# A planned RWKV + MLP kernel: new planner constants, a charge for changing the kind of matmul, and the diagonal terms of four units on GpSimd

## The chip, the cores and the metric

The kernel runs on one core of one Trainium2 chip. The metric is the device time of one execution in microseconds, smaller is better; the median of three runs of the kernel before is 541.37 us (541.27 to 541.45).

## The reference

An RWKV recurrence over 768 tokens (batch 4, 8 heads, head size 48), and behind it an MLP with an ELU in the middle (384 to 2048 to 384) on the 3072 tokens that come out.

```python
for t in range(S):
    cur = np.einsum('bhd,bhe->bhde', u[None] * kt, vt)
    y[:, :, t] = np.einsum('bhd,bhde->bhe', rt, state + cur)
    state = wt[:, :, :, None] * state + np.einsum('bhd,bhe->bhde', kt, vt)
...
h = x @ w_in
g = np.where(h > 0.0, h, alpha * (np.exp(np.minimum(h, 0.0)) - 1.0))
return g @ w_out
```

## The kernel before, in words

The sequence is cut into 6 chunks of 128 tokens; a chunk and a batch make a unit, so there are 24 units, 0 to 23, four to a chunk (units 0 to 3 are chunk 0, units 4 to 7 chunk 1, and so on). The units of chunks 2, 3 and 4 work in two halves of 64 tokens (HALVES).

A unit's attention is a chain of steps over all engines. VectorE makes two running products of the decays (`es`, `gs`: L377, L387) and scales r and k with them (`rh`, `kh`: L392, L396). The diagonal term, the sum of r times k times u for each head and token, becomes the small tile `md`. It is made in one of two ways. With DIAG "PE", VectorE multiplies r by k (`rkc`, L416), TensorE sums with u by small matmuls (`pd`, L421), ScalarE copies the sum out (`md`, L425). With DIAG "POOL", another copy of r and k by token (`rk`, 384 KB a unit) is loaded, GpSimd multiplies r by k and by u (L404, L407), and VectorE sums for each head (`md`, L411). Then `md` is spread on a diagonal (`sp`): on ScalarE for units 0 to 7 (L432), on GpSimd for the others (L442). TensorE makes the scores (`s`, L456), VectorE lays them over the diagonal (`mk`, L460), TensorE transposes k (`t`, L465; ScalarE copies it out, `kt`, L469), makes the outputs (`v`, L493 to L506; `ya` is the part of it that takes the state) and the state's update (`u`, L532), VectorE brings the state up to date (`sc`, `up`: L472, L540, L542), and the output is split in a high and a low part for fp32r matmuls (`xh`, `xl`: L513, L519).

The MLP goes by chunk and by f, the 16 blocks of 128 hidden units: `g1` (9 matmuls of 512 columns, L238), ReLU and exponential on ScalarE (L243, L246), ELU on VectorE (`stt`, L249), the split (`gh` L253 on ScalarE, `gl` L257 on VectorE), and `g2` (9 matmuls, L268). In chunks 0 and 1 the first six f are done in two halves of 256 columns. Each f needs its weights once, in a high and a low part: they are loaded in chunk 0 and worked up by ScalarE and VectorE (`a`, `cand`, `cb`, `cc`, `wh`, `wl`: L559 to L577).

The order on every engine's queue is written down at build time by `Plan.order()`, a list scheduler. Each step has an assumed duration (COST), and a latest time `late`, which runs backwards from due times: `g1` and `g2` of chunk c are due along the line from BEGINS[c] to BEGINS[c+1], and `v` of a unit at BEGINS[c] less STAG (half units) or STAG_C (others, chunks 2 and up) for each unit of its chunk that follows. At each moment every engine takes, of the steps that are ready and whose buffers are free, the one with the smallest `late` (L143). STAY is added to a step of TensorE if it would change between attention and MLP, SWITCH to the time that TensorE is taken when the kind of step changes (L168), and HALF is a time up to which TensorE is assumed at half speed (L166). `lock` says that VectorE and GpSimd are assumed not to run such steps at once. Only the order goes into the kernel; on the chip each queue waits by semaphores. Scores take two of three PSUM tiles "pa" until `mk`, `u` of a half unit two of them until `up2` and `xl` (L707, L713); the loads of a chunk's units may start LEAD before BEGINS (L599).

Of the kernel before, what the change touches and what calls it, by code (L numbers as in the profile page):

```python
# [8 lines left out]
F32 = mybir.dt.float32  # L9
# [4 lines left out]
AF = mybir.ActivationFunctionType  # L14
ALU = mybir.AluOpType
# [35 lines left out]
PIECES = _pieces()  # L51


COST = dict(es=1.5, gs=1.4, pc=0.2, pd=0.6, md=0.22, spa=2.4, rh=0.62, kh=0.62, rk=0.48, rku=0.48, prk=1.1, prku=1.1, dg=0.5, mk=0.7, up=0.7, sc=0.5, xl=0.48,
            cand=0.5, cv=0.9, wl=0.9, stt=0.6, gl=0.64, fl=1.4, kt=0.5, xh=0.46, a=0.87, wh=0.8, r1=0.58, r2=0.6, gh=0.6,
            sp=1.7, s=1.15, t=0.5, v=1.75, v0=1.1, u=0.5, g=2.06, out=0.6, sh=0.6, ya=0.4, vh=1.0)
LAT = 0.06
DMA_FIRST, DMA_ISSUE, DMA_LAT, DMA_RATE = 1.0, 0.45, 1.9, 215.0
BEGINS = (20.9, 120.4, 207.5, 284.8, 361.5, 453.5, 461.1)
SOON = 0.0  # L60
HALF = 0.0
STAY = 0.0
SWITCH = 0.0
MODES = dict(s=1, v=2, u=3, pd=4)
STAG = 10.9
STAG_C = 0.0
HALVES = (2, 3, 4)
FIRST = "DVE"
FILL = {}
COLS = 128  # L70
PAD = 96
LEAD = 69.5
DIAG = ["PE"] * 8 + ["POOL"] * 16
SPREAD = ["ACT"] * 8 + ["POOL"] * 16
SLOTS = dict(w=2, k=3, r=3, rk=2, v=4, eg=2, md=2, am=2, kt=1, pa=3, wg=2, ph=2, m=2, gh=2, gl=2, x=2, acc=1, raw0=1, x0=1, x1=1, x1a=1, x1b=1)

# [1 line left out]
class Plan:  # L78
# [5 lines left out]
    def add(self, key, eng, dur, fn, after=(), due=None, start=0.0, lock=False, size=0):  # L84
        self.tasks[key] = dict(key=key, eng=eng, dur=dur, fn=fn, after=list(after), due=due, start=start, lock=lock, size=size)
# [8 lines left out]
    def order(self):  # L94
# [14 lines left out]
        for k in reversed(topo):  # L109
            t = ts[k]  # L110
# [4 lines left out]
        users = {}  # L115
        ring = {p: [0, [False] * n] for p, n in SLOTS.items()}
        free = lambda p, n: not any(ring[p][1][(ring[p][0] + x) % len(ring[p][1])] for x in range(n))
        ready = {e: [] for e in ("PE", "DVE", "ACT", "POOL", "SP")}
        count = {k: len(t["after"]) for k, t in ts.items()}
        at = {k: t["start"] for k, t in ts.items()}  # L120
        rank = {k: n for n, k in enumerate(ts)}
# [2 lines left out]
        server, mode = DMA_FIRST, None  # L124
# [5 lines left out]
        while len(order) < len(ts):  # L130
            moved = False
            for e in ready:
                if busy[e] > now + 1e-9:
                    continue
                best = None
                for k in ready[e]:
                    t = ts[k]
                    if at[k] > now + 1e-9 or any(
                            not free(p, n) or (p in turn and turn[p][0] != k) for p, n, _ in self.holds.get(k, ())):
                        continue  # L140
                    if t["lock"] and max(v for x, v in locked.items() if x != e) > now + 1e-9:
                        continue
                    u = (t["late"] + (STAY if e == "PE" and (k[0] in MODES) != (mode in MODES) else 0.0), rank[k])  # L143
                    if best is None or u < best[0]:
                        best = u, k
                if best is None:
                    continue
                k = best[1]
                t = ts[k]
                ready[e].remove(k)  # L150
                for p, n, us in self.holds.get(k, ()):
                    at_, n_ = ring[p][0], len(ring[p][1])
                    ring[p][0] = (at_ + n) % n_
# [12 lines left out]
                end = now + t["dur"] * (2.0 if e == "PE" and now < HALF else 1.0)  # L166
                if e == "PE":
                    end += SWITCH * (MODES.get(mode, 0) != MODES.get(k[0], 0))  # L168
                    mode = k[0]
                busy[e] = end  # L170
                if t["lock"]:
                    locked[e] = end
                if e == "SP":
                    server = max(server, end) + t["size"] / DMA_RATE / 1e3
                    end = server + DMA_LAT
                t["began"], t["ended"] = now, end
                events.append((end, k))
                order.append(k)
                moved = True
# [112 lines left out]
def rwkv_elu_kernel(ctx, tc, wkr, rk, vp, u, uz, gkrw, gv, gu, w_in, w_out, out):  # L292
    nc = tc.nc
# [16 lines left out]
    tt, stt, act = nc.vector.tensor_tensor, nc.vector.scalar_tensor_tensor, nc.scalar.activation  # L310
# [4 lines left out]
    w_h = big.tile([P, NF, 2, NK, P], F32R, name="w_h")  # L315
    w_l = big.tile([P, NF, 2, NK, P], F32R, name="w_l")
# [16 lines left out]
    raws, xts = {}, {}  # L333
# [253 lines left out]
    add, hold, K = plan.add, plan.hold, COST  # L587
# [9 lines left out]
    for u_ in units:  # L597
# [44 lines left out]
            after.append(("v", i - 1))  # L642
        more = 0.15 * u_["half"]
        if u_["half"]:
            add(("u", i), "PE", K["u"], lambda u_=u_: outer(u_), [("kt", i)] + after[:3])
            add(("ya", i), "PE", K["ya"], lambda u_=u_: state_part(u_, 0), [("u", i), ("sc", i)])
            add(("up", i), "DVE", K["up"], lambda u_=u_: update(u_), [("ya", i)])
            add(("sc2", i), "DVE", K["sc"], lambda u_=u_: scale_state(u_, 1), [("up", i)], lock=True)
            add(("v", i), "PE", K["vh"], lambda u_=u_: value(u_), after + [("sc2", i)], due=BEGINS[c] - (B - 1 - b) * STAG - 2.0)
            add(("up2", i), "DVE", K["up"], lambda u_=u_: update(u_, 1), [("xl", i)])  # L650
        else:
            add(("v", i), "PE", K["v" if c else "v0"], lambda u_=u_: value(u_), after, due=BEGINS[c] - (B - 1 - b) * STAG_C - 1.0 if c > 1 else None)
# [5 lines left out]
    for f in range(NF):  # L658
        for z in range(2):
            add(("raw", f, z), "SP", DMA_ISSUE, lambda f=f, z=z: load_w(f, z), [("raw", f, 0)] if z else [("raw", f - 1, 1)], size=393)  # L660
        add(("a", f), "ACT", K["a"], lambda f=f: conv_a(f), [("raw", f, 0), ("raw", f, 1)])
        add(("cand", f), "DVE", K["cand"], lambda f=f: conv_and(f), [("a", f)], lock=True)
        add(("cb", f), "DVE", K["cv"], lambda f=f: conv_b(f), [("cand", f)], lock=True)
        add(("cc", f), "DVE", K["cv"], lambda f=f: conv_c(f), [("cb", f)], lock=True)
        add(("wh", f), "ACT", K["wh"], lambda f=f: conv_h(f), [("cc", f)])
        add(("wl", f), "DVE", K["wl"], lambda f=f: conv_l(f), [("wh", f)], lock=True)
    n0, prev = 0, None
    seq = []
    for c in range(NC):
# [186 lines left out]
```

## Time and profile before

| | |
|---|---|
| median of 3 runs | 541.37 us |
| the profiled execution: its time, its span | 543.14 us, 540.9 us |
| mean granted clock of TensorE | 0.974 |
| busy: TensorE matmuls, weight loads | 515.5 us (95%), 427.7 us (79%) |
| busy: VectorE, ScalarE, GpSimd | 371.1 us (69%), 285.8 us (53%), 74.7 us (14%) |
| chain that ended last, by engine | TensorE 80%, VectorE 9%, DMA 6%, ScalarE 2% |

The execution's own time is 2.24 us over its span. The busy time of TensorE is modelled from the starts of matmuls, so slow or spread-out matmuls count as busy too; how long a group of nine takes from its start to the next start says more. The table is a mean over stages; the rows below show the stages.

### The profile page before, as it was taken

Reading aid. Unit: us, or ns where it says so; the run is one execution under the profiler, and the core shown is the slowest. Engines: PE = TensorE matmul, PEld = TensorE weight load, DVE = VectorE, ACT = ScalarE, POOL = GpSimd, SP = SyncE. Lnnn points to the kernel's source line nnn. Section 1 sums busy time; section 2 is a strip of 40 time slices with the busy share of each in tenths; the row PEclk is TensorE's granted clock in tenths of the full one; section 3 lists DMA queues with packets and bytes.
Section 4 is the critical chain, followed back from the end, with each engine's and each line's share of the span. In section 5 each row is a group of like instructions: output and inputs, shape, how many; then the busy total and the mean of one; then the engine's idle time right before and its main releaser. Section 6 shows DMA issues by size and latency. Waiting matters only on the chain.

```text
span 540.9 us, 12202 instructions
## 1 busy us (share of the span) xinstructions
PE 515.5 (95%) x5121; PEld 427.7 (79%) x5121; DVE 371.1 (69%) x614; ACT 285.8 (53%) x570; POOL 74.7 (14%) x102
## 2 busy tenths in 40 slices
PE   6876999989999999999999999999999999999994
PEld 5666998878999777787777788777788887888883
DVE  5899899988778875469964478964436995333331
ACT  3768588675855453455453365543355543454441
POOL 2000000000243120028120035120031400000000
PEclk9977899979999999999999999999999999999998
DMA  8954754021562200094310083100084110010001
GB/s 243 287 176 141 226 175 164 19 56 35 175 178 76 65 2 2 2 263 133 85 33 2 3 241 103 35 2 3 1 254 124 48 35 2 0 60 0 1 0 63
DMA packets 26749, 47.54 MB, mean 88 GB/s; under 512 B 2753, under 2 KB 9281, under 8 KB 26689
## 3 DMA queue, kind: packets, MB, share of 16 engines
q1 hardware_dynamic: 26544, 46.58, 28.7%
q8 instruction: 42, 0.69, 0.5%
q14 instruction: 19, 0.15, 0.1%
q10 hardware_dynamic: 144, 0.13, 0.1%
HBM read 41.98 MB, written 4.72 MB: 86 GB/s over the span
## 4 chain that ended last, share of the span: by engine, by line
PE 80%; DVE 9%; DMA 6%; ACT 2%; issue 1%; SPq 0%; DVEq 0%; ACTq 0%
PE ph L238 34%; PE acc L268 33%; PE pa_s L456 3%; PE pa_y L501 3%; DMA v<-in_vp_dram 3%; PE pa_u L506 2%; PE pa_u L493 2%; PE pa_u L532 1%; DMA wrawx<-in_w_out_dram 1%; DMA rk<-in_rk_dram 1%; PE pa_t L465 1%; DVE eg L387 1%; DVE gl L257 1%; DMA k<-in_wkr_dram 1%; DVE r L392 1%
## 5 line engine op out<-in xcount | busy, mean ns | idle before, releaser
L243 ACT ACTIVATE m<-ph 128x512 f32<-128x512 f32 (+1 forms) x108 | 59.2, 549 | 132.8 <-PE ph L238 131.5
L249 DVE SCALAR_TENSOR_TENSOR m<-m,ph 128x512 f32<-128x512 f32 (+1 forms) x108 | 67.4, 624 | 84.7 <-ACT m L246 84.2
L238 PE MATMUL ph<-xh,w_h 128*128 128x512 f32 (+1 forms) x324 | 123.2, 380 | 2.0 <-ACT w_h L574 1.6
L238 PE MATMUL ph<-xh,w_l 128*128 128x512 f32 (+1 forms) x324 | 120.7, 372 | 3.7 <-DVE w_l L577 3.7
L268 PE MATMUL acc<-gh,w_h 128*128 128x512 f32 (+1 forms) x325 | 123.6, 380 | 0.0
L268 PE MATMUL acc<-gl,w_h 128*128 128x512 f32 (+1 forms) x325 | 120.2, 370 | 0.1
L238 PE MATMUL ph<-xl,w_h 128*128 128x512 f32 (+1 forms) x324 | 120.1, 371 | 0.0
L268 PE MATMUL acc<-gh,w_l 128*128 128x512 f32 (+1 forms) x325 | 119.9, 369 | 0.0
L257 DVE TENSOR_TENSOR gl<-m,gh 128x512 fp32r<-128x512 f32 (+1 forms) x108 | 73.2, 681 | 36.4 <-ACT gh L253 35.9
L253 ACT CAST gh<-m 128x512 fp32r<-128x512 f32 (+1 forms) x108 | 61.5, 571 | 55.9 <-DVE m L249 33.2
L238 PEld LDWEIGHTS ph<-xh,w_l 128*128 128x128 f32 x324 | 62.3, 192 | 15.0 <-DVE w_l L577 4.6
L238 PEld LDWEIGHTS ph<-xh,w_h 128*128 128x128 f32 x324 | 62.2, 192 | 14.3 <-ACT w_h L574 2.4
L268 PEld LDWEIGHTS acc<-gh,w_h 128*128 128x128 f32 x325 | 62.4, 192 | 12.8 <-issue 1.0
L268 PEld LDWEIGHTS acc<-gh,w_l 128*128 128x128 f32 x325 | 62.4, 192 | 10.2
L268 PEld LDWEIGHTS acc<-gl,w_h 128*128 128x128 f32 x325 | 62.5, 192 | 9.7 <-DVE gl L257 0.5
L238 PEld LDWEIGHTS ph<-xl,w_h 128*128 128x128 f32 x324 | 62.5, 193 | 9.4
L246 ACT ACTIVATE m<-m 128x512 f32<-128x512 f32 (+1 forms) x108 | 63.3, 586 | 2.9
L442 POOL TENSOR_SCALAR_AFFINE_SELECT am<-md 64x256 f32<-64x256 f32 (+1 forms) x56 | 30.5, 548 | 96.9 <-PE pa_u L493 61.9
L404 POOL TENSOR_TENSOR rk<-rk 128x384 f32<-128x384 f32 x16 | 19.1, 1192 | 134.1 <-DMA rk<-in_rk_dram 132.2
L377 DVE TENSOR_TENSOR_SCAN eg<-w,reset 112x516 f32<-112x516 f32 (+1 forms) x24 | 31.0, 1292 | 2.6 <-DMA w<-in_wkr_dram 2.6
L456 PE MATMUL pa_s<-r,k 48*64 48x64 f32 (+1 forms) x576 | 27.3, 262 | 5.5 <-ACT md L425 2.2
L401 ACT ACTIVATE junk<-eg,lim 112x1032 bf16<-112x1032 f32 (+1 forms) x24 | 27.7, 1153 | 8.2 <-DVE eg L387 8.2
(72 smaller groups left out, 513.4 us busy)
## 6 DMA issues: line engine op xcount, KB each, us to landing
v<-in_vp_dram SPq DMA_DIRECT2D x24, 256.0 KB, 6.5
rk<-in_rk_dram SPq DMA_DIRECT2D x16, 384.0 KB, 4.1
w<-in_wkr_dram SPq DMA_DIRECT2D x24, 227.9 KB, 3.9
k<-in_wkr_dram SPq DMA_DIRECT2D x24, 224.0 KB, 4.9
r<-in_wkr_dram SPq DMA_DIRECT2D x24, 224.0 KB, 5.3
out_dram<-o SPq DMA_DIRECT2D x17, 256.0 KB, 2.5
wrawx<-in_w_in_dram SPq DMA_DIRECT2D x10, 384.0 KB, 3.5
wrawx<-in_w_out_dram SPq DMA_DIRECT2D x10, 384.0 KB, 4.1
```

Source lines behind the costliest of these rows:

```text
L238: nc.tensor.matmul(ph[z:z + COLS], w[:, f, 0, k, z:z + COLS], x_[:, k, :], start=(k == n == 0), stop=(k == NK - 1 and n == 2))
L243: act(s["m"], s["ph"], AF.Relu, scale=-1.0)
L246: act(s["m"], s["m"], AF.Exp, scale=-1.0)
L249: stt_(s["m"], s["m"], -1.0, s["ph"], ALU.add, ALU.max)
L253: nc.scalar.copy(s["gh"], s["m"])
L257: nc.vector.tensor_tensor(s["gl"], s["m"], s["gh"].bitcast(F32), ALU.subtract)
L268: nc.tensor.matmul(a_[z:z + COLS], w[:, f, 1, m, z:z + COLS], g[:, s_], start=(f == n == 0 and lo == 0), stop=(f == NF - 1 and q == parts ...
L377: nc.vector.tensor_tensor_scan(out=eg[:, 0, 0:n][:, ::-1], data0=u_["w"][:, 1:n + 1][:, ::-1], data1=reset[:, 0, 0:n][:, ::-1], initial=0. ...
L401: act(junk[:, :, 0:n], u_["eg"][:, :, 0:n], AF.Relu, bias=lim, accum_out=flags[:, u_["i"]:u_["i"] + 1])
L404: eng.tensor_tensor(u_["rk"][:, 0], u_["rk"][:, 0], u_["rk"][:, 1], ALU.mult)
L442: nc.gpsimd.affine_select(out=am[rs, :, 0:L], in_=u_["md"][rs, q::2].unsqueeze(2).broadcast_to([L, NP, L]), pattern=[[0, NP], [1, L]], com ...
L456: nc.tensor.matmul(pa[q][ts, p, 0:L], u_["k"][rs, p, ts], u_["r"][rs, p, ts], start=True, stop=True)
```

## The change

Every constant of COST is set anew, mostly lower, and half units get their own value for `u` (`uh`). BEGINS moves (chunk 0 from 20.9 to 28.6, chunks 1 to 4 earlier by 2.5 to 7.5, chunk 5 later by 1.6). HALF goes from 0 to 17, STAY from 0 to 2, SWITCH from 0 to 0.1, and a new term OUTSIDE of 0.08 is charged at a change between attention and MLP; `ya` and `t` now count as attention. STAG goes from 10.9 to 8.4, STAG_C from 0 to 14. DIAG is "PE" for units 0 to 3 only, so units 4 to 7 go the way of GpSimd, with SPREAD still on ScalarE. A second way to make `wl` is added and not used, since BY_DMA is empty.

```diff
-COST = dict(es=1.5, gs=1.4, pc=0.2, pd=0.6, md=0.22, spa=2.4, rh=0.62, kh=0.62, ... prk=1.1, prku=1.1, dg=0.5, mk=0.7, up=0.7, sc=0.5, xl=0.48,
-            cand=0.5, cv=0.9, wl=0.9, stt=0.6, gl=0.64, fl=1.4, kt=0.5, xh=0.46, a=0.87, wh=0.8, r1=0.58, r2=0.6, gh=0.6,
-            sp=1.7, s=1.15, t=0.5, v=1.75, v0=1.1, u=0.5, g=2.06, out=0.6, sh=0.6, ya=0.4, vh=1.0)
+COST = dict(es=1.3, gs=1.45, pc=0.15, pd=0.95, md=0.15, spa=2.4, rh=0.61, kh=0.61, ... prk=1.0, prku=1.1, dg=0.48, mk=0.65, up=0.72, sc=0.48, xl=0.48,
+            cand=0.5, cv=0.88, wl=0.88, stt=0.6, gl=0.62, fl=1.2, kt=0.45, xh=0.45, a=0.83, wh=0.75, r1=0.57, r2=0.57, gh=0.55,
+            sp=1.6, s=0.95, t=0.4, v=1.6, v0=0.95, u=0.4, uh=0.45, g=2.045, out=0.6, sh=0.55, ya=0.38, vh=0.9)
-BEGINS = (20.9, 120.4, 207.5, 284.8, 361.5, 453.5, 461.1)
+BEGINS = (28.6, 117.8, 205.0, 279.8, 354.0, 455.1, 455.7)
-HALF = 0.0
-STAY = 0.0
-SWITCH = 0.0
-MODES = dict(s=1, v=2, u=3, pd=4)
-STAG = 10.9
-STAG_C = 0.0
+HALF = 17.0
+STAY = 2.0
+SWITCH = 0.1
+MODES = dict(s=1, v=2, ya=2, u=3, pd=4, t=5)
+OUTSIDE = 0.08
+STAG = 8.4
+STAG_C = 14.0
+BY_DMA = ()
-DIAG = ["PE"] * 8 + ["POOL"] * 16
+DIAG = ["PE"] * 4 + ["POOL"] * 20
...
-                    end += SWITCH * (MODES.get(mode, 0) != MODES.get(k[0], 0))
+                    end += SWITCH * (MODES.get(mode, 0) != MODES.get(k[0], 0)) + OUTSIDE * ((mode in MODES) != (k[0] in MODES))
...
-            add(("u", i), "PE", K["u"], lambda u_=u_: outer(u_), [("kt", i)] + after[:3])
+            add(("u", i), "PE", K["uh"], lambda u_=u_: outer(u_), [("kt", i)] + after[:3])
```

## Rows read from the trace of the kernel before

**Rows 1.** The page: the span in 40 equal slices (13.5 us each), busy tenths of VectorE.

```profile
DVE  5899899988778875469964478964436995333331
```

**Rows 2.** Stretches of the span: us; busy time (and instructions) of TensorE matmuls, weight loads, VectorE, ScalarE, GpSimd; granted clock; DMA share; GB/s.

```profile
26.00:64.00 38.00, 29.95 (x257) 26.34 (x258) 35.15 (x58) 24.93 (x56) 0.00 (x0) 0.78 0.52 165
64.00:110.00 46.00, 46.00 (x258) 40.37 (x257) 44.92 (x68) 34.98 (x62) 0.00 (x0) 1.00 0.40 131
110.00:130.00 20.00, 17.82 (x214) 15.35 (x213) 16.51 (x27) 12.13 (x32) 0.00 (x0) 0.83 0.23 61
130.00:224.00 94.00, 94.00 (x1351) 79.92 (x1350) 69.49 (x135) 52.12 (x122) 20.10 (x28) 1.00 0.24 72
...
388.00:460.00 72.00, 72.00 (x553) 58.61 (x552) 48.83 (x70) 35.06 (x64) 14.84 (x16) 1.00 0.29 87
```

**Rows 3.** TensorE in order of time where chunk 0 ends: start, duration, line, tiles, shapes, count, idle before and what ended it.

```profile
110.13 1.84 PE L421 MATMUL pa_d<-ubd,rkc 112*128 112x2 f32 x16
111.90 0.56 PE L532 MATMUL pa_u<-v,kt 128*48 128x48 f32 x16
114.65 2.08 PE L456 MATMUL pa_s<-r,k 48*128 48x128 f32 x16 [2.18 <-ACT md L425]
116.66 0.79 PE L238 MATMUL ph<-xh,w_h 128*128 128x512 f32 x1
...
120.45 0.39 PE L268 MATMUL acc<-gh,w_h 128*128 128x512 f32 x1
```

**Rows 4.** VectorE in order of time over the same place.

```profile
107.14 0.68 DVE L416 TENSOR_TENSOR rkc<-r,k 112x512 f32<-112x512 f32 x1
...
110.57 1.21 DVE L377 TENSOR_TENSOR_SCAN eg<-w,reset 112x516 f32<-112x516 f32 x1
112.52 0.72 DVE L542 COPY st<-pa_u 48x192 f32<-48x192 f32 x2 [0.74 <-PE pa_u L532]
113.25 0.69 DVE L392 TENSOR_TENSOR r<-r,eg 112x512 f32<-112x512 f32 x1
113.86 0.68 DVE L396 TENSOR_TENSOR k<-k,eg 112x512 f32<-112x512 f32 x1
114.47 0.95 DVE L577 TENSOR_TENSOR w_l<-wg,w_h 128x768 fp32r<-128x768 f32 x1
...
124.21 1.36 DVE L460 COPY_PREDICATED am<-upper,pa_s 128x512 f32<-128x512 uint32 x2 [1.88 <-PE pa_s L456]
```

**Rows 5.** TensorE in order of time in chunk 1: the first matmul of its first `g1`, and the place about the `pd` of units 6 and 7.

```profile
129.50 0.28 PE L238 MATMUL ph<-xh,w_h 128*128 128x256 f32 x1
...
134.79 1.84 PE L421 MATMUL pa_d<-ubd,rkc 112*128 112x2 f32 x16
136.49 0.37 PE L238 MATMUL ph<-xh,w_h 128*128 128x256 f32 x1
```

**Rows 6.** The chain of work that ended last, in order of time (start, duration, what): one half unit of chunk 2 among MLP groups of chunk 1. The left-out pieces are the other attention matmuls of the visits.

```profile
177.56 0.38 PE pa_t L465 x4
177.94 0.62 PE pa_s L456 x32
178.57 2.29 PE acc L268 x9
180.86 0.51 PE pa_u L532 x32
...
181.84 2.29 PE ph L238 x9
...
185.38 2.28 PE acc L268 x9
187.66 2.06 PE ph L238 x9
```

**Rows 7.** The same chain in chunks 0 and 1: a half-width MLP group between others of its kind, and two that stand beside attention.

```profile
64.63 1.08 PE acc L268 x9
...
145.38 1.26 PE acc L268 x9
146.65 1.67 PE pa_y L501 x56
148.32 1.26 PE acc L268 x9
```

**Rows 8.** GpSimd, groups of instructions by shape: count, busy time and mean ns of one, idle before and what ended it.

```profile
L407 POOL TENSOR_TENSOR rk<-rk,ub 128x384 f32<-128x384 f32 x16 | 20.4, 1276 | 1.3
L404 POOL TENSOR_TENSOR rk<-rk 128x384 f32<-128x384 f32 x16 | 19.1, 1192 | 134.1 <-DMA rk<-in_rk_dram 132.2 <-DVE md L411 1.7
```

**Rows 9.** GpSimd in order of time where it works beside VectorE.

```profile
254.04 1.47 POOL L404 TENSOR_TENSOR rk<-rk 128x384 f32<-128x384 f32 x1
255.58 1.34 POOL L407 TENSOR_TENSOR rk<-rk,ub 128x384 f32<-128x384 f32 x1
```

**Rows 10.** VectorE over the same time, with the sum for a diagonal in it.

```profile
254.55 1.50 DVE L392 TENSOR_TENSOR r<-r,eg 112x512 f32<-112x512 f32 x1
...
259.65 0.54 DVE L411 TENSOR_REDUCE md<-rk 128x8 f32<-128x384 f32 x1
```

**Rows 11.** The page's DMA issues: what, queue, count, KB each, median us from issue to landing.

```profile
rk<-in_rk_dram SPq DMA_DIRECT2D x16, 384.0 KB, 4.1
```

**Rows 12.** One more stretch, columns as in rows 2: the time in which the loads of chunk 1 begin.

```profile
50.00:60.00 10.00, 7.99 (x70) 6.81 (x69) 8.75 (x15) 4.31 (x8) 0.00 (x0) 0.66 0.94 290
```

More of the change, by code (lines that the diff above doesn't have):

```diff
@@ L51 @@
 PIECES = _pieces()
-COST = dict(es=1.5, gs=1.4, pc=0.2, pd=0.6, md=0.22, spa=2.4, rh=0.62, kh=0.62, rk=0.48, rku=0.48, prk=1.1, prku=1.1, dg=0.5, mk=0.7, up=0.7, sc=0.5, xl=0.48,
-            cand=0.5, cv=0.9, wl=0.9, stt=0.6, gl=0.64, fl=1.4, kt=0.5, xh=0.46, a=0.87, wh=0.8, r1=0.58, r2=0.6, gh=0.6,
-            sp=1.7, s=1.15, t=0.5, v=1.75, v0=1.1, u=0.5, g=2.06, out=0.6, sh=0.6, ya=0.4, vh=1.0)
+COST = dict(es=1.3, gs=1.45, pc=0.15, pd=0.95, md=0.15, spa=2.4, rh=0.61, kh=0.61, rk=0.48, rku=0.48, prk=1.0, prku=1.1, dg=0.48, mk=0.65, up=0.72, sc=0.48, xl=0.48,
+            cand=0.5, cv=0.88, wl=0.88, stt=0.6, gl=0.62, fl=1.2, kt=0.45, xh=0.45, a=0.83, wh=0.75, r1=0.57, r2=0.57, gh=0.55,
+            sp=1.6, s=0.95, t=0.4, v=1.6, v0=0.95, u=0.4, uh=0.45, g=2.045, out=0.6, sh=0.55, ya=0.38, vh=0.9)
 LAT = 0.06
 DMA_FIRST, DMA_ISSUE, DMA_LAT, DMA_RATE = 1.0, 0.45, 1.9, 215.0
-BEGINS = (20.9, 120.4, 207.5, 284.8, 361.5, 453.5, 461.1)
+BEGINS = (28.6, 117.8, 205.0, 279.8, 354.0, 455.1, 455.7)
 SOON = 0.0
-HALF = 0.0
-STAY = 0.0
-SWITCH = 0.0
-MODES = dict(s=1, v=2, u=3, pd=4)
-STAG = 10.9
-STAG_C = 0.0
+HALF = 17.0
[6 more added lines that the diff above has]
+BY_DMA = ()
 HALVES = (2, 3, 4)
@@ L117, in order @@
         free = lambda p, n: not any(ring[p][1][(ring[p][0] + x) % len(ring[p][1])] for x in range(n))
-        ready = {e: [] for e in ("PE", "DVE", "ACT", "POOL", "SP")}
+        ready = {e: [] for e in ("PE", "DVE", "ACT", "POOL", "SP", "NET")}
         count = {k: len(t["after"]) for k, t in ts.items()}
@@ L574, in conv_h, with conv_n, conv_d @@
         nc.scalar.copy(w_h[:, f], raws[f][1].bitcast(F32))
+    def conv_n(f):
+        act(w_l[:, f], w_h[:, f].bitcast(F32), AF.Copy, scale=-1.0)
+    def conv_d(f):
+        nc.gpsimd.dma_start(w_l[:, f].bitcast(F32), raws[f][1].bitcast(F32), accum_op=ALU.add)
     def conv_l(f):
@@ L665, in rwkv_elu_kernel @@
         add(("wh", f), "ACT", K["wh"], lambda f=f: conv_h(f), [("cc", f)])
-        add(("wl", f), "DVE", K["wl"], lambda f=f: conv_l(f), [("wh", f)], lock=True)
+        if f in BY_DMA:
+            add(("wn", f), "ACT", 0.75, lambda f=f: conv_n(f), [("wh", f)])
+            add(("wd", f), "POOL", 1.0, lambda f=f: conv_d(f), [("wn", f)])
+            add(("wl", f), "NET", 4.5, lambda: None, [("wd", f)])
+        else:
+            add(("wl", f), "DVE", K["wl"], lambda f=f: conv_l(f), [("wh", f)], lock=True)
     n0, prev = 0, None
```

## The prediction

> **What bounds the kernel now.** Start with the stretches [rows 2], because the page's table is a mean over stages with different limits. From 130 us on TensorE is busy without a gap and at full clock (94.00 of 94 us to 224, 72.00 of 72 from 388 to 460). There only two things make the kernel shorter: less work on TensorE, or the same work in fewer pieces. Ahead of 130 us it is another kernel. From 26 to 64 us TensorE is busy for 29.95 of 38 us, at a granted clock of 0.78, while VectorE is busy for 35.15 us; from 64 to 110 us VectorE works for 44.92 of 46 us; the slices of the page show its 9s there and nowhere later [rows 1, 2]. VectorE works up sixteen blocks of weights in this front part, beside the attention of chunks 0 and 1, and what TensorE lacks is fed by VectorE. TensorE is full from 64 to 110 us only because the half-width groups have filled a stock of MLP work; at 110 us the stock is used up.
>
> Next comes the place where chunk 0 ends [rows 3]. TensorE does `pd` of two units for 1.77 us (110.13 to 111.90), then `u`, waits 2.18 us, does `s` of unit 4 at the slow clock (2.08 us, about half of it lost), and then a `g1` that takes 3.79 us (116.66 to 120.45) where an undisturbed one takes 2.06 [rows 6]. That is 2.18 + 1.0 + 1.73 = 4.9 us of loss. The row puts the wait down to `md`, but VectorE's queue shows what came last [rows 4]: it waited 0.74 us for `u`, which stood behind `pd` on TensorE; only then did it scale r and k, up to 114.54, and `s` began at 114.65. The last block's `wl` stood behind that again, and the slow `g1` needs it.
>
> **The change part by part.** The diff gives a new order on all queues, and what that order is can't be read off the diff. So parts with an answer in rows are summed first, and the rest gets bounds.
>
> *`pd` of units 6 and 7.* It stands in the part that TensorE bounds [rows 5]: 136.49 - 134.79 = 1.70 us. It also cuts an MLP stretch: a half-width group beside attention takes 1.26 us instead of 1.08 [rows 7], 0.18 us for a visit. Together -1.9 us. ScalarE's two copies go too; ScalarE has room there (52.12 of 94 us [rows 2]).
>
> *`pd` of units 4 and 5.* Its 1.77 us lies just ahead of a wait, so it is not gained as such. If the order stays as it is, `u` starts 1.77 us earlier, VectorE's wait of 0.74 us goes, and the next limit is the scan that ends at 111.78 [rows 4]. VectorE loses `rkc` (0.61 us of its queue, as the product of the same shape from 113.25 to 113.86) and gains the sum for the diagonal (0.54 us [rows 10]); with three units in the front part that is 3 x 0.07 = 0.2. Together -0.9 us on the front part.
>
> *The new order of the front part.* VectorE's idle time from 26 to 130 us is 2.85 + 1.08 + 3.49 = 7.4 us [rows 2]; 0.7 of it is counted above, and 1.88 us more stands in one wait for `s` at 124.21 [rows 4]. At best the new order saves the other 6.7; at worst it saves nothing, or makes a wait such as the one at 110 us somewhere else (up to 4.9 again). The assumed durations now lie near the rows (a full group 2.045 against 2.06), BEGINS puts chunk 1's attention earlier against chunk 0's weights (due 2.6 us earlier, chunk 0 7.7 us later), and this is the conflict at 110 us [rows 3, 4]. But the queues are in order, and an assumed time a little too short (`wl` 0.88 against 0.95) makes an engine wait for another. I take a bit less than half: -3.0 us, bounds 0 and -6.7.
>
> *GpSimd beside VectorE.* Units 4 to 7 add two products each on GpSimd, eight instructions of 1.2 to 1.3 us mean [rows 8]. No GpSimd work of this kind stands in the front part of the trace, so the price comes from later: the scaling of r took 1.50 us while GpSimd multiplied [rows 9, 10] and 0.69 us while it rested [rows 4]. That is 0.81 us of VectorE for one product, where VectorE reads two tiles from SBUF. Eight times that is 6.5 us, if all stand in the front part and all collide; the other bound is 0, if they run beside work that does not collide or after 130 us. I take four that stand in the front part with half the price: +1.6 us. The Trainium skill (SBUF — State Buffer, "Who interferes with whom") states that a VectorE instruction with two SBUF inputs and a GpSimd instruction that reads SBUF lock each other out for the whole of one instruction, the later one waiting. The trace agrees in kind; the 0.81 us is less than the 1.34 and 1.47 us of the products beside it [rows 9]. By the rule taken to its end the eight would cost VectorE about 9.9 us at their means [rows 8], and the sum would be -1.6 instead of -4.9 if the four that I count waited in full.
>
> *The loads.* Four `rk` loads of 384 KB come onto SP's queue, among the weights and chunk 1's w, k, r and v. At the 290 GB/s of the fullest stretch [rows 12] one is 1.36 us of transfer, and it lands in 4.1 us [rows 11]. From 64 to 110 us the DMA share is 0.40, so there they are hidden and I take 0. If two stand from 50 to 60 us, where the share is 0.94, the weights behind them come up to 2.7 us later; that is the upper bound, and what then waits is the first pass over the weights on ScalarE, and VectorE behind it.
>
> *Fewer changes of kind.* A half unit visits TensorE three times, t and s, u and ya, ya and v, and after each visit an MLP group takes 2.29 us instead of 2.06 [rows 6]: 0.23 us. Twelve half units make 36 visits, 8.3 us. STAY can't merge them: `u` needs `mk` of the same unit from VectorE, `v` the state that `ya` releases, and `s` of the next unit needs two PSUM tiles that `u` holds until the `xl` of its own unit. So 0 there. Chunk 1 and chunk 5 have whole units, which hold fewer tiles. At most two visits for each of chunk 1's four units could merge, 8 x 0.18 = 1.4; I take half, -0.7 us, bounds 0 and -1.4.
>
> *HALF and the first 26 us.* The planner now believes a slow TensorE until 17 us. I see no row that this moves in one direction, and take 0; a changed order there costs or gains what VectorE's queue does, and is held by the bounds above.
>
> **The sum.** -1.9 - 0.9 - 3.0 + 1.6 - 0.7 = -4.9 us. The profiled execution took 543.14 us for a span of 540.9 and goes to 538.2; it stands 1.77 us above the median of the runs, so against the median 541.37 the forecast is 536.5 us.
>
> **The rivals.** *The front part closes.* The new order saves all 6.7 us of VectorE's idle time, the products on GpSimd meet nothing, and visits merge to their bound: -1.9 - 0.9 - 6.7 - 1.4 = -10.9, 530.5 us. For it: the idle time stands in a few waits with a name. Against it: VectorE would be full for 100 us in order, with three other engines in its chain.
>
> *Slower: GpSimd takes VectorE's time where VectorE is the bound.* All eight products collide ahead of 130 us, and the new order saves no other idle time: -1.9 - 0.9 - 0.7 + 6.5 = +3.0, 544.4 us. It decides from about four full collisions on (3.5 / 0.81). For it: from 64 to 110 us VectorE's queue is full, most of it with steps on weights that read two tiles from SBUF (L567, L571, L577), and the planner's `lock` orders the plan but holds nothing back on the chip. Against it: loads and due times may put units 6 and 7 after 130 us, as `pd` of these units is now. By the page's full lockout the same case ends at about 548 us.
>
> *The stall only moves.* The order is different but has a wait of its own, the size of the one before `s`, 2.2 us [rows 3], in place of the saved idle time: -1.9 - 0.9 + 1.6 - 0.7 + 2.2 = +0.3, 541.7 us. The change then does not do what it says. With the full 4.9 us it would be 544.4.
>
> **How the numbers follow.** The forecast has 0.50, with a range of its own from 533.1 (idle time -5.0, collisions +0.5, visits -1.0) to 539.8 (-1.0, +2.5, -0.3). The front part closing has 0.20, GpSimd as the bound 0.15, the moved stall 0.10; 0.05 is left for loads in the way or something I don't see, half of it slower. A measurement of this kernel can tell about 0.2% from no change, 540.3 to 542.5. Faster: 0.50 + 0.20 + 0.02 = 0.72; within: 0.10 + 0.01 = 0.11; slower: 0.15 + 0.02 = 0.17. The range of 8 in 10 reaches halfway into the first rival and up to most of the second: 531.0 to 543.5.
>
> **What would show it.** Right: no `pd` in chunk 1; the first `g1` of chunk 1 earlier than 129.50 us [rows 5] by 2 to 3 us, with VectorE's idle time from 26 us to there below 6 us; from there to the end about 2.6 us shorter; still three visits for each half unit. The rival of GpSimd shows as products on GpSimd ahead of 110 us with VectorE's instructions of 0.68 and 0.95 us stretched beside them, and the first `g1` of chunk 1 later than now. The moved stall shows as a new wait of TensorE over 2 us with a slow clock behind it. The prediction is wrong in its base if TensorE has gaps after 130 us, or if half units need fewer or more visits.

## The result and the profile after

The changed kernel takes 544.66 us, the kernel before 541.66 us beside it on the same chip (medians of 10 runs each): ratio 1.0052, 95% interval 1.0027 to 1.0077. It is slower by 0.5%, about 2.8 us, where 4.9 us of gain were forecast, and lies outside the range.

The profiled execution took 546.85 us for a span of 545.1 us and stands 2.2 us above the median, so sizes below come from medians, and its trace is used for places and durations. Its lines are two further down (eight from the weights' `wl` on): `md` on ScalarE is L427, the scores `s` L458, `conv_a`, the first pass over a weight block, L561.

The slices of VectorE and the five stretches, columns as in [rows 1, 2]:

```profile
DVE  5789999998869955588755799354548785333331
```

```profile
26.00:64.00 38.00, 31.97 (x304) 27.53 (x304) 33.80 (x54) 26.78 (x62) 3.17 (x3) 0.91 0.54 167
64.00:110.00 46.00, 44.98 (x313) 39.39 (x313) 44.61 (x69) 36.10 (x69) 3.97 (x3) 1.00 0.54 168
110.00:130.00 20.00, 15.62 (x76) 12.51 (x76) 18.41 (x26) 10.75 (x24) 2.32 (x2) 0.83 0.14 43
130.00:224.00 94.00, 92.63 (x1312) 79.33 (x1310) 71.35 (x133) 53.33 (x123) 23.28 (x29) 1.00 0.33 101
388.00:460.00 72.00, 72.00 (x594) 59.18 (x596) 47.73 (x74) 36.36 (x66) 15.48 (x16) 1.00 0.31 87
```

The picture of [rows 2] holds: VectorE is busiest in the front, and TensorE has no gap from 388 to 460 us. The 1.37 us that TensorE lacks from 130 to 224 us is one wait, ahead of `s` of unit 8 at 164.70, which the kernel before does not have. The slices say less than the prediction took from them: 9s of VectorE stand behind the front too, here from 164 to 191 us, in the kernel before from 243 to 270 us [rows 1], to name one place each. What moved is the hand-over. TensorE in order of time, where chunk 0 ends, and the first `g1` of chunk 1:

```profile
115.82 0.39 PE L270 MATMUL acc<-gh,w_l 128*128 128x512 f32 x1
120.59 2.08 PE L458 MATMUL pa_s<-r,k 48*128 48x128 f32 x16 [4.38 <-issue]
122.59 0.79 PE L270 MATMUL acc<-gh,w_h 128*128 128x512 f32 x1
...
126.60 0.60 PE L240 MATMUL ph<-xh,w_h 128*128 128x512 f32 x1
...
139.10 0.28 PE L240 MATMUL ph<-xh,w_h 128*128 128x256 f32 x1
```

The stall of [rows 3] is still there: the wait ahead of `s` of unit 4 is 4.38 us (2.18 before), `s` takes 2.0 us again, the group behind it 4.01 us (122.59 to 126.60). Chunk 1's first `g1` starts at 139.10, against 129.50 [rows 5]; from there to the end of the span it is 406.0 us against 411.4. So the front part lost 9.6 us in this trace and the rear won 5.4.

Why the wait doubled shows in VectorE's queue over the same place, and in GpSimd's:

```profile
116.47 1.21 DVE L379 TENSOR_TENSOR_SCAN eg<-w,reset 112x516 f32<-112x516 f32 x1
117.59 1.49 DVE L394 TENSOR_TENSOR r<-r,eg 112x512 f32<-112x512 f32 x1
119.00 1.48 DVE L398 TENSOR_TENSOR k<-k,eg 112x512 f32<-112x512 f32 x1
120.41 0.68 DVE L259 TENSOR_TENSOR gl<-m,gh 128x512 fp32r<-128x512 f32 x1
121.01 0.94 DVE L585 TENSOR_TENSOR w_l<-wg,w_h 128x768 fp32r<-128x768 f32 x1
```

```profile
117.54 1.00 POOL L406 TENSOR_TENSOR rk<-rk 128x384 f32<-128x384 f32 x1 [41.22 <-DMA rk<-in_rk_dram]
118.61 1.32 POOL L409 TENSOR_TENSOR rk<-rk,ub 128x384 f32<-128x384 f32 x1
```

The scaling of r and k of unit 4 takes 1.49 and 1.48 us, where [rows 4] has 0.69 and 0.68, just while GpSimd makes the two products of unit 7; `s` starts at 120.59, when the scaling of k has ended (120.48). That is 1.60 us for two products, 0.80 each, the price taken from [rows 9, 10]. All eight products ran ahead of chunk 1's first `g1`.

The new wait at 164.70 looks the same way: the scaling of r and k of unit 8 is stretched beside two more products, and `s` follows when it has ended (164.60). VectorE, GpSimd, TensorE:

```profile
161.86 1.34 DVE L394 TENSOR_TENSOR r<-r,eg 112x512 f32<-112x512 f32 x1
163.12 1.48 DVE L398 TENSOR_TENSOR k<-k,eg 112x512 f32<-112x512 f32 x1
```

```profile
161.64 1.01 POOL L409 TENSOR_TENSOR rk<-rk,ub 128x384 f32<-128x384 f32 x1
162.60 1.44 POOL L406 TENSOR_TENSOR rk<-rk 128x384 f32<-128x384 f32 x1
```

```profile
164.70 0.69 PE L458 MATMUL pa_s<-r,k 48*64 48x64 f32 x32 [1.37 <-issue]
```

The wait stands, with 1.36 to 1.38 us, in the trace of every version below that has the changed constants, except e9. No run moved or shortened these products, so its price is not shown.

The second loss is at the start. ScalarE, then TensorE, in order of time:

```profile
12.64 0.18 ACT L403 ACTIVATION_READ_ACCUMULATOR junk<-eg,lim 112x1 f32 x1
20.29 0.89 ACT L561 ACTIVATE wg<-wrawx 128x768 f32<-128x768 f32 x1 [7.46 <-DMA wrawx<-in_w_out_dram]
...
22.94 0.16 ACT L427 COPY md<-pa_d 128x8 f32<-128x8 f32 x1
```

```profile
14.07 0.98 PE L467 MATMUL pa_t<-ident,k 112*128 112x112 f32 x4 [1.81 <-issue]
23.16 0.79 PE L458 MATMUL pa_s<-r,k 48*128 48x128 f32 x2 [8.10 <-ACT md L427]
```

In ScalarE's queue `conv_a` of the second weight block now stands ahead of `md` of unit 0. It waits 7.46 us for its load, `md` waits behind it, and TensorE waits 8.10 us for `md`. With HALF at 17 the planner doubles the assumed time of the warm-up matmuls and of `pd` of unit 0. In the plan that `Plan.order()` makes, the load of that block ends at 10.55 us; `pd` of unit 0 ends at 9.45 us with HALF 0 and at 14.40 us with HALF 17, so that `conv_a` is ready ahead of `md`. On the chip the wait for the load ended at 20.29 us. HALF brings the step forward, and a load that is planned some 10 us too early makes it wait.

### The profile page after: what moved, and what is told of

The parts are those of the page before. It is cut to its first block, busy times and chain, and to the rows that moved or that the text cites. A ratio compares the mean times of both kernels' runs of the same rounds, so it can differ in the third digit from the quotient of the medians.

```text
span 545.1 us, 12144 instructions
## 1 busy us (share of the span) xinstructions
PE 508.5 (93%) x5089; PEld 420.3 (77%) x5089; DVE 372.7 (68%) x614; ACT 286.2 (53%) x566; POOL 83.0 (15%) x110
## 4 chain that ended last, share of the span: by engine, by line
PE 81%; DVE 8%; DMA 5%; ACT 3%; issue 2%; SPq 0%; ACTq 0%
PE acc L270 33%; PE ph L240 33%; PE pa_s L458 4%; PE pa_y L503 3%; PE pa_u L508 2%; PE pa_u L534 2%; PE pa_t L467 2%; PE pa_u L495 2%; DVE gl L259 1%; DMA v<-in_vp_dram 1%; DMA wrawx<-in_w_out_dram 1%; DVE eg L389 1%; DMA w<-in_wkr_dram 1%; DMA k<-in_wkr_dram 1%; DVE wg L569 1%
## 5 line engine op out<-in xcount | busy, mean ns | idle before, releaser
L240 PE MATMUL ph<-xh,w_h 128*128 128x512 f32 (+1 forms) x324 | 121.7, 376 | 1.4 <-DVE m L251 1.4
L240 PE MATMUL ph<-xl,w_h 128*128 128x512 f32 (+1 forms) x324 | 118.8, 367 | 0.4 <-DVE xl L521 0.4
L240 PE MATMUL ph<-xh,w_l 128*128 128x512 f32 (+1 forms) x324 | 118.7, 366 | 0.2 <-DVE w_l L585 0.2
L240 PEld LDWEIGHTS ph<-xh,w_h 128*128 128x128 f32 x324 | 61.3, 189 | 13.5 <-DVE m L251 2.4
L270 PEld LDWEIGHTS acc<-gl,w_h 128*128 128x128 f32 x325 | 61.9, 190 | 10.8 <-DVE gl L259 1.3
L240 PEld LDWEIGHTS ph<-xh,w_l 128*128 128x128 f32 x324 | 61.1, 188 | 10.6 <-DVE w_l L585 0.4
L240 PEld LDWEIGHTS ph<-xl,w_h 128*128 128x128 f32 x324 | 61.3, 189 | 10.0 <-DVE xl L521 0.8
L444 POOL TENSOR_SCALAR_AFFINE_SELECT am<-md 64x256 f32<-64x256 f32 (+1 forms) x56 | 28.4, 510 | 172.1 <-PE pa_u L495 93.6
L406 POOL TENSOR_TENSOR rk<-rk 128x384 f32<-128x384 f32 x20 | 25.2, 1258 | 157.8 <-DMA rk<-in_rk_dram 157.7
L458 PE MATMUL pa_s<-r,k 48*64 48x64 f32 (+1 forms) x576 | 27.5, 262 | 19.0 <-ACT md L427 9.9
L458 PEld LDWEIGHTS pa_s<-r,k 48*64 48x64 f32 (+1 forms) x576 | 22.7, 167 | 26.6 <-issue 12.9
```

What stands on the lines that cost most here:

```text
L240: nc.tensor.matmul(ph[z:z + COLS], w[:, f, 0, k, z:z + COLS], x_[:, k, :], start=(k == n == 0), stop=(k == NK - 1 and n == 2))
L270: nc.tensor.matmul(a_[z:z + COLS], w[:, f, 1, m, z:z + COLS], g[:, s_], start=(f == n == 0 and lo == 0), stop=(f == NF - 1 and q == parts ...
L406: eng.tensor_tensor(u_["rk"][:, 0], u_["rk"][:, 0], u_["rk"][:, 1], ALU.mult)
L444: nc.gpsimd.affine_select(out=am[rs, :, 0:L], in_=u_["md"][rs, q::2].unsqueeze(2).broadcast_to([L, NP, L]), pattern=[[0, NP], [1, L]], com ...
L458: nc.tensor.matmul(pa[q][ts, p, 0:L], u_["k"][rs, p, ts], u_["r"][rs, p, ts], start=True, stop=True)
```

## The experiments

Each kernel was timed beside the kernel before, on the same chip; ratios are to before, with 95% intervals, and the difference of two of the closer ones has an interval of about 0.35% (1.9 us) to each side. "VectorE" is its busy time and its idle time from 10 us to chunk 1's first `g1`, by the row of that stretch in each trace; these are single executions, and with the same order at the start (e1, e7, e8, e12) the idle time goes from 6.68 to 8.95 us.

| kernel | ratio (interval) | VectorE busy, idle, us |
|---|---|---|
| before | 1 | 109.22, 10.28 |
| changed | 1.0052 (1.0027 to 1.0077) | 117.26, 11.84 |
| e1: changed, HALF 0 | 0.9991 (0.9967 to 1.0015) | 115.41, 6.68 |
| e3: before, HALF 17 | 1.0096 (1.0062 to 1.0130) | 109.52, 13.63 |
| e5: changed, short products | 1.0013 (0.9992 to 1.0033) | 113.78, 11.53 |
| e7: HALF 0 and short products | 0.9951 (0.9927 to 0.9975) | 113.38, 8.03 |
| e6: second `conv_a` behind unit 0's spread | 0.9990 (0.9970 to 1.0009) | 115.88, 7.25 |
| e8: HALF 0, unit 7's products later | 0.9954 (0.9930 to 0.9978) | 115.16, 8.95 |
| e12: e8, unit 5's `es` later | 0.9987 (0.9962 to 1.0013) | 115.38, 8.22 |
| e10: e8, early steps of units 6, 7 later | 1.0035 (1.0014 to 1.0056) | |
| e11: e10, scores of unit 6 later | 1.0111 (1.0080 to 1.0143) | |
| e4: before, units 4 to 7 on GpSimd | 1.0222 (1.0192 to 1.0252) | |
| e9: HALF 0, no charges for a change | 1.0190 (1.0148 to 1.0232) | |

Two theories stood against each other: that the start (HALF) costs the time, or that VectorE's work in the front part does (GpSimd's products, and the order).

**e1 and e3: HALF alone, taken out and put in.**

```diff
-HALF = 17.0
+HALF = 0.0
```

> The changed kernel with HALF back at 0; all else of the change stays. In the changed kernel the first g1 starts at 37.92 us (26.69 before), because ScalarE's first pass over the second weight block stands ahead of md of unit 0 and waits 7.46 us for its load. Theory of the start (the late first g1 is most of the loss): the first g1 comes at about 27 us, the first g1 of chunk 1 about 7 us earlier than 139.1, and the time falls by 6 to 9 us, to 536 to 539. Theory of VectorE's work (the start is mostly hidden, since VectorE bounds all the time ahead of chunk 1 and its idle time there grew by only 1.9 us, 15.2 to 17.1): the first g1 comes early too, but the time falls by only about 2 us, to 543.

> The kernel before with HALF at 17 and nothing else. Theory of the start: ScalarE's second weight step goes ahead of md of unit 0, the first g1 comes about 10 us later, and the time rises by 6 to 9 us, to 548 to 551. Theory of VectorE's work: the first g1 comes as late, but the time rises by about 2 us, to 543 to 544.

Measured: e1 is 0.61% below the changed kernel (3.3 us), e3 5.2 us above the one before. Both are in between what the two theories gave: HALF costs more than the whole loss, and less than the start shows in the trace. In e1, ScalarE has `md` ahead of the load again:

```profile
11.39 0.14 ACT L427 COPY md<-pa_d 128x8 f32<-128x8 f32 x1
...
17.79 0.93 ACT L561 ACTIVATE wg<-wrawx 128x768 f32<-128x768 f32 x1 [0.90 <-DMA wrawx<-in_w_out_dram]
```

The first `g1` of all starts at 26.56 us there and at 37.92 in the changed kernel: 11.4 us, of which by the medians 3.3 reach the end. What passes through is nearer to VectorE's waiting at the start: from 10 to 40 us it is idle for 6.6 to 7.1 us in the traces of the changed kernel, e3 and e5, and for 0.9 to 4.0 us in those of before, e1, e7, e8 and e12. The wait on TensorE is refilled, most of the time that VectorE lost is not.

**e5 and e7: GpSimd's products cut short, with HALF at 17 and at 0.**

```diff
-        eng.tensor_tensor(u_["rk"][:, 0], u_["rk"][:, 0], u_["rk"][:, 1], ALU.mult)
+        n = 8 if u_["c"] == 1 else DM
+        eng.tensor_tensor(u_["rk"][:, 0, 0:n], u_["rk"][:, 0, 0:n], u_["rk"][:, 1, 0:n], ALU.mult)
```

(and the product with u in the same way)

> The changed kernel with the products of r, k and u on GpSimd cut to 8 of 384 columns for units 4 to 7; the rest of their diagonal terms is then left out of the computation. No queue's order changes. It prices the collisions of GpSimd with VectorE ahead of chunk 1 by themselves: VectorE's stretched steps there (two of 1.49 and 1.48 instead of 0.69 at 117.59, one of 1.38 instead of 0.56 and one of 1.65 instead of 0.95 at 63 to 65, and some gl) add up to 3.4 us. If VectorE bounds the front, the time falls by 2 to 3.5 us, to 541 to 543; if only the pair at 117.59 stands where it matters, by 1.6 to 2.5; under the theory of the start it falls by less than 1.

> The changed kernel with HALF 0, and the GpSimd products of units 4 to 7 cut to 8 of 384 columns (it leaves out most of the diagonal terms of chunk 1; the order of the steps stays). Theory that the two costs are separate: HALF's 3.3 us and the collisions' 2.1 us add, the time is 5.4 us below the changed kernel, 539.3 with before at 542.1 (ratio to before 0.995). Rival (both costs go into the same place, the end of chunk 0 where VectorE's queue is full, so that either alone is hidden by the other): no more than 3.5 us below, 541 to 542.

Measured: the four ratios make a square. HALF costs 0.61% with full products (1.0052 - 0.9991) and 0.62% with short ones (1.0013 - 0.9951); the products cost 0.39% (1.0052 - 1.0013) and 0.40% (0.9991 - 0.9951). So 3.3 us and 2.1 us, each with an interval of some 1.3 us to each side, and they add: together they are 1.01% (5.5 us, 3.6 to 7.4), over the 3.5 us of the rival. e5's 2.1 us alone fits both VectorE's whole time and the one pair at 117.59; e8 parts these. Without either cost the change is 2.65 us faster than before (0.49% of 541.8).

**e6: the start's mechanism, with HALF left at 17.** One dependency in the planner:

```diff
+    plan.tasks[("a", 1)]["after"].append(("sp", 0))
```

> The changed kernel with HALF left at 17, and one dependency more in the planner: the first pass over weight block 1 on ScalarE (conv_a) comes behind the spread of unit 0, so that unit 0's md doesn't stand behind a weight block that isn't there yet. From chunk 1 on the planned order is that of the changed kernel. Theory of the start (HALF costs its 3.3 us only because unit 0's chain waits behind the load of block 1 on ScalarE): s of unit 0 near 15 us instead of 23.2, first g1 near 27 us instead of 37.9, and the time 2.5 to 4 us below the changed kernel, at 541 to 542.5 with before at 542.1. Rival (HALF costs through its other effects, the longer plan of the warm-up matmuls and of the MLP's first groups): less than 1 us gained, 544 to 545.

Measured: 541.51 us, in the middle of the theory's range; all that HALF costs is back. The picture was not as expected: `s` of unit 0 came at 22.84 us, not near 15, because `md` now stands behind the first block's `wh`:

```profile
18.37 0.83 ACT L576 CAST w_h<-wg 128x768 fp32r<-128x768 f32 x1 [2.47 <-DVE wg L573]
19.11 0.16 ACT L427 COPY md<-pa_d 128x8 f32<-128x8 f32 x1
```

TensorE's scores are as late as in the changed kernel, and yet the time is that of e1. What did change is VectorE's idle time: 7.25 us, against 11.84; from 10 to 40 us 3.5 against 6.65. So the place of this one step carries the price of HALF, and TensorE's 8.10 us of waiting are not that price. That it is VectorE's waiting is read from the traces; no run changes that alone.

**e8: unit 7's products later, with HALF 0.** The order is changed by hand when the planner has made it:

```diff
+        order = plan.order()
+        moved = [t for t in order if t["key"] in (("ld_rk", 7), ("rk", 7), ("rku", 7))]
+        order = [t for t in order if t not in moved]
+        n = [t["key"] for t in order].index(("ld_w", 7)) + 1
+        order[n:n] = moved
```

> The changed kernel with HALF 0 and the load and the two GpSimd products of unit 7 moved by hand further back in the order, behind the load of w of chunk 1's last unit, so that they no longer run beside the scaling of r and k of unit 4, for which the first g1 of chunk 1 waits. All work is done. Theory of the collisions at one place (the two of unit 7, 0.8 us each, lie on the way to the first scores of chunk 1, the other six have slack): 1 to 1.6 us below the changed kernel with HALF 0 alone, 540 to 540.5 with before at 542.1. Rival (VectorE's whole time in the front part counts, wherever a collision lies): the products collide with other steps instead, within 0.5 us of HALF 0 alone, 541.1 to 542.

Measured: 540.24 us, and by the ratios 0.37% (2.0 us) below e1, a little more than expected, with intervals of some 1.3 us on each. It gives back what all short products gave in e7, so, as far as the intervals tell, the price of the products stands at this one place. This version is faster than both kernels. r and k of unit 4 are scaled undisturbed, and the products meet only the end of a scan:

```profile
115.61 0.67 DVE L394 TENSOR_TENSOR r<-r,eg 112x512 f32<-112x512 f32 x1
116.20 0.69 DVE L398 TENSOR_TENSOR k<-k,eg 112x512 f32<-112x512 f32 x1
...
127.45 1.51 DVE L379 TENSOR_TENSOR_SCAN eg<-w,reset 112x516 f32<-112x516 f32 x1
```

```profile
116.98 1.16 PE L458 MATMUL pa_s<-r,k 48*128 48x128 f32 x16 [2.81 <-issue]
```

The price shows at this place in the traces too. From the start of the wait before `s` of unit 4 to chunk 1's first `g1` it is 22.9, 22.1 and 21.8 us where unit 7's full products run beside the scaling (changed, e1, e6), and 19.9 us in each of e5, e7 and e8: some 2 to 3 us. One or two stretched steps make 0.8 to 1.6 of it. The rest goes with the clock of TensorE: over the 7 us from the start of `s` the granted clock is 0.54 to 0.58 in the first three, after waits of 3.6 to 4.4 us, and 0.76 in the others, after 2.8; `s` takes 2.0 us against 1.1. (In before it is 0.60 after a wait of 2.2 us, so the length of the wait alone does not set it.)

A wait of 2.81 us before `s` of unit 4 is left, though; the next runs ask whether it can be ordered away.

**e10 and e11: steps that the new order brought forward, moved back.** With `behind` moving the named steps in the order:

```diff
+        behind([("es", 6), ("md", 7), ("gs", 6), ("pc", 6), ("fl", 6)], ("xl", 5))
+        behind([("es", 7)], ("kh", 6))
```

```diff
+        behind([("s", 6), ("mk", 6, 0), ("mk", 6, 1)], ("g1", 24))
```

> The changed kernel with HALF 0 and unit 7's products moved as in the run before, and the early steps of chunk 1's units 6 and 7 that the new order brought ahead of chunk 1's first g1 on VectorE (es and md, gs of unit 6; es of unit 7; about 4.2 us) moved by hand behind the last xl of unit 5, the es of unit 7 behind kh of unit 6. TensorE's order stays. All work is done. Theory that the front part ends when VectorE's queue lets it, and that these steps took back the gain of the new order: the last gl of chunk 0 and chunk 1's first g1 come about 3 us earlier, nothing waits behind them, and the time is 1 to 2.5 us below the run without this, ratio to before 0.991 to 0.9935. Rival (the steps have to be done ahead of the scores of unit 6 anyway, which stand two groups further on in TensorE's queue): the first g1 comes earlier but TensorE waits 1 to 3 us at those scores, and the time is the same, ratio 0.9945 to 0.9965, or above.

> As the run with the steps moved back, and the scores of unit 6 and their masks stand one MLP group further back in the order, behind the third g1 of chunk 1. All work is done. Theory of VectorE's queue as the end of the front part: the wait at the scores of unit 6 is gone or under 1 us, ratio to before 0.991 to 0.9935. Rival (the order of the steps about the first g1 moves no time): 0.9945 to 0.9965, with the wait in another place.

Measured: both slower than e8, by 0.8 and 1.6%. In e10 the rival's mechanism shows, and it costs more than the rival gave: counted from `s` of unit 4, chunk 1's first `g1` comes 16.2 us later instead of 17.1 in e8, and then TensorE stops 0.96 us at `s` of unit 6 and 1.76 us at the third `g1`, which waits for an `stt` that stands behind the moved scans.

```profile
138.01 1.16 PE L458 MATMUL pa_s<-r,k 48*128 48x128 f32 x16 [0.96 <-PE ph L240]
...
141.43 0.58 PE L240 MATMUL ph<-xh,w_h 128*128 128x256 f32 x1 [1.76 <-DVE m L251]
```

From there to the end of the span e10 takes 410.2 us, e8 405.9. The theory that these steps took back the gain of the order falls. In e11 TensorE waits 3.88 us at the `g1` that waited 1.76 in e10, ahead of the moved scores; what the rest of its loss is was not followed up.

**e12: one step moved from before the wait to behind it.**

```diff
+        behind([("es", 5), ("pc", 5)], ("wl", 15))
```

> The changed kernel with HALF 0 and unit 7's products moved (as in the run that is faster than both kernels), and one more step moved by hand: the running product es of unit 5 (1.21 us) goes behind the last block's wl on VectorE; it stands now between gs and the scaling of r of unit 4, for which TensorE waits with the scores of unit 4 (2.81 us in that run). All work is done. Theory that the wait before the scores of unit 4 is the order of VectorE's queue there and that the front part ends with it: the wait is 1.2 us shorter and the time 0.7 to 1.2 us lower than in that run, ratio to before 0.993 to 0.9945. Rival (VectorE has no idle time there, so that the step only moves the wait to what comes behind): the wait at the scores is shorter, but the next ones, or the last groups of chunk 0, come as late as before, ratio 0.995 to 0.9965.

Measured: 0.9987, no gain. TensorE's waits for scores, of unit 4 and of unit 5:

```profile
114.99 1.16 PE L458 MATMUL pa_s<-r,k 48*128 48x128 f32 x16 [1.82 <-issue]
...
122.65 1.16 PE L458 MATMUL pa_s<-r,k 48*128 48x128 f32 x16 [1.78 <-issue]
```

The first is 1.0 us shorter than in e8, and a new one of 1.78 us stands before the scores of unit 5, which e8 started without one. The moved scan is work that VectorE has to do ahead of them, in a queue without room: from the start of the first wait to chunk 1's first `g1` it is 20.4 us, against 19.9 in e8. The ratio is also above e8's by 0.3%. In this trace unit 7's products cost VectorE more: a scan beside them took 1.95 us (1.51 in e8), and the sum for the diagonal behind it waited 0.84 us for the second product, which it did not in e8. The intervals of the two ratios overlap, and whether this is the reason stays open.

**e4: units 4 to 7 on GpSimd in the kernel before, old constants.**

```diff
-DIAG = ["PE"] * 8 + ["POOL"] * 16
+DIAG = ["PE"] * 4 + ["POOL"] * 20
```

> The kernel before with the diagonal terms of units 4 to 7 on GpSimd and nothing else; the planner makes a new order from it. Theory of the start: it keeps its early first g1, loses pd of four units (1.9 us behind 130 us), and is 1 to 3 us faster, 539 to 541. Theory of VectorE's work: the products stand in the front and collide, and it is 1 to 4 us slower, 543 to 546.

Measured: 12 us slower than before. With the old constants the planner takes `s` of unit 8 early and then holds back chunk 2's units; the stretch between the first `g1` of chunks 1 and 2 grows from 94.5 to 105.4 us. The run tells of that order, not of the products.

**e9: the charges for a change of kind at 0, with HALF 0.**

```diff
-STAY = 2.0
-SWITCH = 0.1
-OUTSIDE = 0.08
+STAY = 0.0
+SWITCH = 0.0
+OUTSIDE = 0.0
```

> The changed kernel with HALF 0 and with the three terms for a change of kind at 0 (STAY, SWITCH, OUTSIDE); all else stays. Theory that the charge for changes joined the visits of chunks 1 and 5 and made the rear shorter (3.4 us net, of which 1.7 is pd): visits of chunk 1 go back to about 20, and the time rises by 1 to 2 us over HALF 0 alone, 542.5 to 543.5. Rival (the charge only moves the order, and the shorter rear comes from pd that is gone and from BEGINS): within 0.5 us of HALF 0 alone, 541 to 542. A planner that no longer waits with attention may also leave a long wait at the end of a chunk; then it is over 545 and tells nothing of the charge itself.

Measured: 10.8 us slower than e1. The visits between the first `g1` of chunks 1 and 2 go from 18 back to 20, as expected. But this order also leaves TensorE waiting in chunk 5's attention (the stage from chunk 4's first `g1` to chunk 5's is 5.6 us longer than in e1), and that price can't be told from the charge's:

```profile
452.01 1.16 PE L458 MATMUL pa_s<-r,k 48*128 48x128 f32 x16 [3.38 <-issue]
```

## Why the prediction was wrong, step by step

| term of the sum | predicted, us | measured, us | from |
|---|---|---|---|
| `pd` of units 6, 7 and fewer changes of kind | -2.6 | -2.4 | rear of the traces |
| `pd` of units 4, 5 and the new order | -3.9 | about -0.2 | what is left of the 2.65 us, not to be told from 0 |
| GpSimd beside VectorE | +1.6 | +2.1 | e5, e7 |
| HALF and the first 26 us | 0 | +3.3 | e1, e7 |
| sum | -4.9 | +2.8 | |

Of the 7.7 us between the two sums, the new order and `pd` of units 4 and 5 make 3.7, HALF 3.3, GpSimd 0.5.

*The step that failed first is the last of the list:* "I see no row that this moves in one direction, and take 0", held "by the bounds above". e1 and e7 price it at 3.3 us, e3 at 5.2 us in the kernel before, and e6 shows the way: one step in ScalarE's queue, put ahead of unit 0's chain, waits for a load. The question that was left out is what a later assumed time of one engine does to the order of another. With the warm-up and `pd` of unit 0 assumed twice as long, `md` becomes ready later, and whatever is assumed ready before it is put ahead, here a step whose load comes late. In the trace of before that step stood behind unit 0's chain, so no row shows its wait there. But the planner stands in the kernel's file, and the order can be computed from it without the chip: the plan with HALF 17 has `conv_a` of block 1 at 10.61 us and `md` of unit 0 at 15.19. It also has all eight products ahead of chunk 1's first `g1` (the last ends at 109.66, the `g1` starts at 122.7).

*The second is the new order, -3.0.* It was to save VectorE's idle time, and with HALF at 0 it did in part: 6.68 us in e1 and 8.03 in e7, against 10.28. The time did not follow. The wait before `s` of unit 4 stayed (2.81 us in e8, where the products no longer disturb it), and e12 shows why: VectorE has next to no idle time there, and a wait that is ordered away comes back before the next scores. VectorE's busy time ahead of chunk 1's first `g1` rose by 4.2 us even with short products (e7 against before), by steps of chunk 1 that used to run behind it, and moving them back by hand made it slower (e10, e11). From the start of the wait before `s` of unit 4 to that `g1` it is 17.0 us in before and 19.9 in e7, longer by about the 3.0 us of work that was moved ahead of it (below). The bound of 0 was nearly the truth. The third rival, "the stall only moves", with a new wait of over 2 us and a slow clock behind it, is what this part of the kernel shows; I gave it 0.10.

*GpSimd.* The mechanism was right and its size a little small, 2.1 us for 1.6, which the interval does not part. The size came by another way than forecast: not from four products at half the price, but from the two of unit 7, at the one place where TensorE waits, and in part by the slower clock behind the longer wait, which the sum did not have. The plan's `lock` keeps the first of these two behind the scaling of k (107.56 us, after 106.06); on the chip it ran with the scaling of r (117.54, 117.59). The rival of GpSimd expected all eight products ahead of chunk 1's first `g1`, and so they were, but they did not all collide. Its time, 544.4 us, is near the one measured for another reason: it had nothing for HALF, and 6.5 us for the products.

*The rear* came near the forecast, in part by luck. Of the 5.4 us by which it is shorter in the traces, 3.0 are work that the new order does ahead of it (one `g2` of 2.04 us, one unit's `t` and `u` of about 0.5 each). The other 2.4 are a difference: TensorE has 3.9 us less to do there, and waits 1.5 us more, 1.37 of them at 164.70. To the 3.9 belong `pd` and visits: no `pd` in chunk 1, 18 visits instead of 20 up to chunk 2's first `g1`, 4 instead of 6 in chunk 5's attention, and in the two stages between them 12 each as before. At the prediction's prices that is about 2.5 us; the rest is not assigned. That STAY can't merge the three visits of a half unit held.

*The base* was sound but for two readings. VectorE's 9s do stand later than 110 us [rows 1], and the wait at 164.70 lies in such a place of the changed kernel: a full VectorE can hold TensorE up there too. And the time outside the span, 2.24 us in the profiled execution, was carried over as fixed. It is 1.7 to 1.9 us in every run of the versions with units 4 to 7 on GpSimd, and 1.9 to 3.2 us in those of the kernel before (median 2.4). So 0.6 us of gain lie outside the span, and inside it `pd` of units 4 and 5 and the new order gained nothing that can be seen. What takes this time is not shown.

*The loads*, taken at 0, show no wait that is theirs apart from the start; no run priced them alone.

*What would show it:* the first `g1` of chunk 1 was to be 2 to 3 us earlier and was 9.6 later, with 8.05 us of idle time on VectorE from 26 us to there instead of under 6; that sign, and the stretched instructions beside GpSimd, were named for the rival.

## What to carry to other kernels

A constant in a planner that makes one engine look slower reorders the other engines' queues too: compute the new order before you forecast, look in it for the steps that wait for a load, and ask which chain they are now put ahead of. Where one engine's queue is full, count its work up to the hand-over and not its waits; moving a step there moves the wait. And place GpSimd's products away from the few VectorE steps for which the bottleneck waits: that was worth 2 us here.

## What the runs showed of the hardware

That a VectorE step with a single input is stretched by GpSimd as well was not in my count. VectorE, then GpSimd, of the changed kernel:

```profile
62.98 1.38 DVE L565 TENSOR_SCALAR wraw<-wraw 128x768 uint32<-128x768 uint32 x1
64.40 1.65 DVE L569 SCALAR_TENSOR_TENSOR wg<-wg,wraw 128x768 uint32<-128x768 uint32 x1
...
68.05 0.56 DVE L565 TENSOR_SCALAR wrawx<-wrawx 128x768 uint32<-128x768 uint32 x1
68.65 0.96 DVE L569 SCALAR_TENSOR_TENSOR wg<-wg,wrawx 128x768 uint32<-128x768 uint32 x1
```

```profile
62.73 1.22 POOL L406 TENSOR_TENSOR rk<-rk 128x384 f32<-128x384 f32 x1
64.02 1.21 POOL L409 TENSOR_TENSOR rk<-rk,ub 128x384 f32<-128x384 f32 x1
```

The `TENSOR_SCALAR` reads one tile and took 1.38 us beside a product, 0.56 us alone; the two-input step behind it 1.65 us and 0.96. In the traces with no full-length product there (before, e3, e5, e7) none of the sixteen such steps took over 0.6 us. The Trainium skill (SBUF — State Buffer, "Who interferes with whom") states that `tensor_scalar` can enter modes that use both of VectorE's ports and can then contend with GpSimd; the trace agrees, by 0.82 us. The granted clock of the front part says little of the time: from 26 to 64 us it is 0.91 in the changed kernel, 0.78 before [rows 2] and 0.63 in e8, the fastest of the three, since TensorE is not what the front part waits for.
